# Agent attention fused with a top-1 mixture of experts: two units of keys, and of values, per block of matmuls

## The chip, the core and the metric

The kernel runs on one core of one Trainium2 chip. The metric is device time in microseconds (us) of one execution; lower is better. A core has five engines that each work through a queue of instructions of their own: TensorE (PE, matmuls; PEld is its loading of weights), VectorE (DVE), ScalarE (ACT), GpSimd (POOL) and SyncE (SP, which issues most DMA transfers). [...] Matmul results land in PSUM, which this kernel uses as eight banks of 512 float32 numbers per partition, and ACT or DVE have to read them out before a bank can be written anew.

## The reference, cut to what matters

Four batches of 11456 tokens with 128 channels go through an attention with 49 agents: the agents attend to the keys and average the values, and the queries attend to the agents. The result, 45824 tokens, is the input of a mixture of eight experts of which each token uses one.

```python
def _attn_ref(q, k, v, agents):              # B, N, C = 4, 11456, 128; 49 agents
    scale = 1.0 / np.sqrt(q.shape[-1])
    a2k = softmax(scale * agents @ k.T)      # over the tokens
    agent_v = a2k @ v
    q2a = softmax(scale * q @ agents.T)      # over the agents
    return q2a @ agent_v

def _moe_ref(x, w_gate, w_output_gate, w1, w2):   # E, D, F = 8, 128, 1024
    logits = x @ w_gate
    e_idx = np.argmax(logits, axis=1)
    gate_w = softmax(logits)[np.arange(N), e_idx]
    eom = 1.0 / (1.0 + np.exp(-(x @ w_output_gate)))
    for e in range(E):
        mask = e_idx == e
        h = np.maximum(x[mask] @ w1[e], 0.0)
        out[mask] = gate_w[mask, None] * eom[mask, e, None] * (h @ w2[e])
```

## The kernel before, in words

**Units.** A batch is cut into twelve units: eleven of 1024 tokens (eight sub-tiles of 128) and a short one of 192 (two sub-tiles of 96). A unit of queries, keys or values is loaded by one DMA of 512 KB (96 KB for the short one) into one of seven places in SBUF, and its place comes free when its matmuls are issued. The order of the loads is the list `ITEMS`, and `small_products` handles the items in this order, each only after the one ahead of it has issued its matmuls.

**Keys and values.** For a unit of keys, eight products with the 49 agents and a column of zeros (50 columns in all) give the scores `ks` in one PSUM bank. ACT copies them to SBUF (`S`), DVE keeps a running maximum. When a batch's twelve units are through, the maximum is known, POOL and ACT make the weights `ev` of one unit after another, and eight products of `ev` with the unit's values give its share `av` in a PSUM bank, which DVE adds to the batch's sum (`avs`). When the last unit is added, the batch's average per agent is folded into the first weight matrix of the expert that most of the batch's tokens use. The products of queries (`qs`) give each token's weights over the agents and, through them, its logits.

**The main products.** A tile is half a unit, 512 tokens. Its first products `h` come in two groups (half 0 and half 1), each of four PSUM banks with eight matmuls: four with 128 rows and four with the rest. ACT makes `hh` of each bank (ReLU in 16 bits) and DVE the remainder `hl`; only when DVE is done is the bank free for the next group. The second products `y` add up 16 pairs of matmuls per bank (eight pieces of `hh`, 256 columns wide, and of `hl`, 128 wide, for two sub-tiles), after which ACT (`ys`) and DVE (`os`) read the bank out, POOL multiplies by the gate and SP stores. Banks 0 to 3 belong to `h`; the other four are shared by `y`, scores, values, logits and all small products. Tokens of another expert than the batch's main one are gathered into 14 left-over tiles (`let`, `lx`, `lh`, `ly`) and scattered over the output by an indirect DMA from POOL.

**The order.** The program is straight-line code that is written in the order that a planner finds when the kernel is built. The planner (`Clock`) keeps a modelled time of each engine and tile. `main_stream` (line 1311) picks the next piece of main work: `mm2`, a pair of `y` matmuls, or `mm1`, a group of `h`; where the model can run neither, `idle`. All other work stands in streams, generators that yield what they need next, and `tick` advances those that can run in the model. A matmul of scores or values is cut into pieces of 32 or 64 columns, which run side by side in the column parts of the array. All pieces of a unit are written as one block (`blocked`, line 491), and a block gets a place only in two cases: behind a group of `h` matmuls (`mm1`, line 1226; pieces of `PART` = 32 columns), or in `idle` (line 510; pieces of 64 columns). At most one block is written at such a place.

**Banks.** `bank` takes of the four shared banks the one whose last reader ends first in the model, `hold` and `release` mark it as taken and free. `wait_free(True)` (line 327), which scores use, keeps one bank free for `y` and lets no more than two banks be held by scores at a time:

```python
            keep = clk.started and (long or not (Y or resting[0]))
            if n_free() > keep and not (long and len(long_held) > 1) and first_free()[0] <= clk.now() + 50.0:
                return
```

Up to the first group of `h`, batch 0's keys and values and the first keys of batch 1 are worked through by single matmuls; blocks come into use with the main products. All instructions that the planner writes have line 217 in the profile (`Engine.emit`), so rows are told apart by the names of their tiles.

Of the kernel before, what the change touches and what calls it, by code (L numbers as in the profile page):

```python
# [18 lines left out]
B, N, C, A, E, F = 4, 11456, 128, 49, 8, 1024  # L19
A2 = 50  # L20
NB = F // P
UNITS = [(u * 1024, 128, 8) for u in range(11)] + [(11264, 96, 2)]
# [122 lines left out]
def _free(x):  # L145
    n = 1
    for k in x.shape[1:]:
        n *= k
    return n
# [117 lines left out]
def agent_attention_top1_moe(ctx, tc, qT, kT, v, aT, wg, wo, w1, w2, cst, out):  # L267
# [3 lines left out]
    PE, SY = Engine(clk, "PE", nc.tensor), Engine(clk, "SP", nc.sync)  # L271
# [12 lines left out]
    last = [0]  # L284
# [5 lines left out]
    def n_free():  # L290
        return sum(banks[k][0] for k in others)
# [4 lines left out]
    def first_free():  # L296
        return min((when_free(banks[k]), k) for k in others if banks[k][0])

    def bank(name, dt=F32, w=512, k=None):

        k = last[0] = first_free()[1] if k is None else k
        t = ps.tile([P, w], dt, tag=f"b{k}", bufs=1, name=name)
        banks[k][1] = t.name
        return t

    def hold(long=False):

        k = last[0]
        banks[k][0] = False
        if long:  # L310
            long_held.append((k, banks[k][1]))
        return k

    def release(k):
        banks[k][0] = True
# [11 lines left out]
    def wait_free(long=False):  # L327
        while True:
            long_held[:] = [x for x in long_held if not banks[x[0]][0] and banks[x[0]][1] == x[1]]
# [4 lines that stand above are left out]
            yield None  # L334
# [6 lines left out]
    at = cp.tile([P, B, A2], F32, name="at")  # L341
# [4 lines left out]
    def load_constants():  # L346
        SY.dma_start(kc, cst)
        SY.dma_start(wgo[:, 0:E], wg)
        SY.dma_start(wgo[:, E:2 * E], wo)
        for t in gss:  # L350
            POOL.tensor_copy(t[:, 0, 16:17], own)
        for t in avt:
            POOL.memset(t, 0.0)
        POOL.tensor_tensor(sel, idf[:, 0:A2], idf[:, 64:64 + A2], op=ALU.add)
# [21 lines left out]
    for i in range(4):  # L376
        t = cp.tile([P, 8, P], F16, name=f"e16_{i}")
        e16s.append(t)
    avd = []
    for i in range(2):  # L380
        t = cp.tile([P, P + 32], F32, name=f"avd_{i}")
# [3 lines left out]
    for i in range(2):  # L385
        t = cp.tile([P, 2, 18], F16, name=f"gs_{i}")
# [3 lines left out]
    for i in range(2):  # L390
        t = cp.tile([P, E, NCOL], F32, name=f"oht_{i}")
# [69 lines left out]
    def spawn(g, prio=2):  # L461
        streams.append([prio, len(streams), g, None])
        streams.sort(key=lambda x: x[0])
# [16 lines left out]
    part = [PART]  # L480
# [7 lines left out]
            if x[3] is not None and x[3][0] == "PE" and clk.can(x[3], x[0]):  # L488
                step(x)

    def blocked(o, pairs, last=None):

        yield "PE", list(pairs[0][1:]), [o], 2
        clk.vt["PE"] += TURN
        n = len(pairs)
        for i, (t, x, m) in enumerate(pairs):
            w = _free(x)
            for h in range(0, w, part[0]):
                c = min(part[0], w - h)
                dst = o[h:h + c, :] if last else o[h:h + c, t * A2:(t + 1) * A2]  # L500
                PE.matmul(dst, x[:, h:h + c], m, start=(not last or i == 0), stop=(not last or i == n - 1))
        clk.vt["PE"] += TURN

    def step(x):
# [24 lines left out]
    parts = {}  # L529
# [26 lines left out]
    def scored(item):  # L556
        places[held.pop(item)][0] = True
# [16 lines left out]
    def loads():  # L574
        for n, item in enumerate(ITEMS):
# [5 lines left out]
            if n == 1:  # L581
                load_constants()

    def scores(item, name):

        kind, b, u = item
        base, pp, nt = UNITS[u]
        while item not in parts or urgent[0] or \
                kind == "k" and b == 1 and u >= EARLY and not clk.started:
            yield None  # L590
        yield from wait_free(True)
        x = parts.pop(item)
        s = bank(name)
        mark = hold(True)
        if clk.started:
            yield from blocked(s, [(t, x[:, t * pp:(t + 1) * pp], at[:, b, :]) for t in range(nt)])
            scored(item)
            return s, mark
        for t in range(nt):
            for h in range(0, pp, 64):  # L600
                w = min(64, pp - h)
                yield from PE.q.matmul(s[h:h + w, t * A2:(t + 1) * A2], x[:, t * pp + h:t * pp + h + w], at[:, b, :],
                                       start=True, stop=True)
        scored(item)
        return s, mark

    NU = len(UNITS)


    K = {}  # L610

    def k_unit(b, u):
        if u == 0:
            K[b] = dict(
                S={},
                mx=wk.tile([P, 8, A2], F32, name=f"mx{b}", tag="mx", bufs=1),
                sm=wk.tile([P, 8, A2], F32, name=f"sm{b}", tag="sme", bufs=1),
                k=0, s=0, v=0, av_n=0,
            )
        s, mark = yield from scores(("k", b, u), f"ks{b}_{u}")  # L620
        spawn(k_rest(b, u, s, mark))

    def k_rest(b, u, s, mark):
        base, pp, nt = UNITS[u]
        S, mx = K[b]["S"], K[b]["mx"]

        n = u
        while K[b]["k"] < n:
            yield None
        sv = s[0:pp, 0:nt * A2]  # L630
        if u // 3 not in S:
            S[u // 3] = wk.tile([P, min(24, NCOL - u // 3 * 24), A2], F32, name=f"S{b}_{u}", tag=f"S{u // 3}", bufs=1)
        Su = S[u // 3][0:pp, u % 3 * 8:u % 3 * 8 + nt, :]
        yield from ACT.q.copy(Su.rearrange("p t a -> p (t a)"), sv)
        release(mark)
        if n > 0:
            yield from DVE.q.tensor_tensor(mx[0:pp, 0:nt], Su, S[0][0:pp, 0:nt, :] if n == 1 else mx[0:pp, 0:nt],
                                           op=ALU.max)
        K[b]["k"] += 1
        if n == NU - 1 or b == 0 and n == FIRST - 1:  # L640
            spawn(k_max(b, n), 1)
# [64 lines left out]
    def v_unit(b, u):  # L706
        base, pp, nt = UNITS[u]
        item = ("v", b, u)
        while b not in K or u not in K[b] or item not in parts:
            yield None  # L710
        if b == 0:
            yield from v_turned(u)
            return
        if u == 0:
            K[b]["av"] = wk.tile([P, A2], F32, name=f"avs{b}", tag="avs")
        yield from wait_free()
        avp = bank(f"av{b}_{u}")
        mark = hold()
        avo = avp[:, 0:A2]
        x = parts.pop(item)  # L720
        e = K[b].pop(u)
        yield from blocked(avo, [(t, x[0:pp, t * C:(t + 1) * C], e[:, t, :]) for t in range(nt)], True)
        scored(item)
        K[b]["v"] += 1
        spawn(v_rest(b, u, avo, mark))

    def v_turned(u):

        base, pp, nt = UNITS[u]
        k0 = K[0]  # L730
        if u in (0, FIRST):
            while not any(banks[k][0] for k in range(G4, 8)):
                yield None
            k = min((when_free(banks[k]), k) for k in range(G4, 8) if banks[k][0])[1]
            k0["avp"] = bank(f"avT{u}", k=k), hold()
        avp, mark = k0["avp"]
        x = parts.pop(("v", 0, u))
        e = k0.pop(u)
        for t in range(nt):
            h = t % 2 * 64  # L740
            yield from PE.q.matmul(avp[h:h + A2, 0:C], e[:, t, :], x[0:pp, t * C:(t + 1) * C],
                                   start=(u in (0, FIRST) and t < 2), stop=(u in (FIRST - 1, NU - 1) and t >= nt - 2))
        scored(("v", 0, u))
        k0["v"] += 1
        if u == NU - 4:
            others[:] = range(G4, 8)
        urgent[0] = u == NU - 1
        if u == FIRST - 1:
            k0["old"] = avp, mark
        if u == NU - 2:  # L750
            spawn(v_copy(0, *k0["old"]), 1)
        if u == NU - 1:
            spawn(shares(), -1)
            spawn(v_last(avp, mark), -1)
# [40 lines left out]
    def v_rest(b, u, avo, mark):  # L795
        av = K[b]["av"]
        while K[b]["av_n"] < u:
            yield None
        if u == 0:
            yield from DVE.q.tensor_copy(av, avo)  # L800
        else:
            yield from DVE.q.tensor_tensor(av, av, avo, op=ALU.add)
        release(mark)
        K[b]["av_n"] += 1
        if u == NU - 1:
            spawn(fold(b), -1)

    def averages(b):
# [391 lines left out]
    MIX = [(3, 0)] * 4 + [(0, 0)] + [(0, 2)] * 6 + [(0, 0)]  # L1200
    ITEMS = order()
    UNIT = {"q": q_unit, "k": k_unit, "v": v_unit}
    EARLY = 3
    FIRST = 8
# [587 lines left out]
```

## Time and profile before

| What | Value |
|---|---|
| Time, median of 3 runs | 982.24 us (982.24 to 983.22) |
| Time of the profiled execution | 981.81 us |
| Its span | 980.0 us |
| Granted clock, mean of the span | 0.995 |
| PE busy | 952.6 us (97%) |
| PEld busy | 729.0 us (74%) |
| DVE busy | 788.2 us (80%) |
| ACT busy | 589.7 us (60%) |
| POOL busy | 355.3 us (36%) |
| Moved by DMA | 148.62 MB, mean 152 GB/s |
| Matmuls of `y` with `hh` / with `hl` | 2880 / 2880 |
| Matmuls of `h` | 1472 |

A profile comes from one execution; its time is compared with that execution's span, and the difference between the two lies around the span. Busy times of engines overlap, so they do not add up to the span. A group row of the profile gives the engine, the operation, the tiles (output, arrow, inputs), the count, the busy time, the mean of one in ns, and, behind the second bar, the idle time just ahead of these instructions with what ended it. A row of the timeline begins with the time from the span's start and the duration; `x8` at its end stands for eight instructions of a kind in a row, and a bracket for a wait ahead of it and its releaser.

### The profile page before, as it was taken

The page shows a single profiled execution, that of the slowest core. Times are in us where ns is not written, and L with a number is a line of the kernel's source. Part 1 is how long each engine was busy: PE and PEld are TensorE (multiplying, and loading weights), DVE is VectorE, ACT ScalarE, POOL GpSimd, SP SyncE. Part 2 cuts the span into 40 slices and gives each one's busy share as a digit, 9 for nine tenths or more (in the row PEclk, how much of TensorE's full clock was granted, in tenths as well). Part 3 has the DMA queues.
Part 4 walks back from the last instruction along what each step waited for, and adds up shares of the span by engine and source line. Part 5 has one row for each costly group of instructions (what it writes and reads, how often), then busy time and mean ns, then how long its engine had stood idle before and what let it go on. Part 6 is the DMA issues. An engine that isn't in the chain of part 4 may idle for free. (4 is left out here: it accounts for less than half of the span.)

```text
span 980.0 us, 37550 instructions
## 1 busy us (share of the span) xinstructions
PE 952.6 (97%) x15740; PEld 729.0 (74%) x15740; DVE 788.2 (80%) x2118; ACT 589.7 (60%) x1400; POOL 355.3 (36%) x630
## 2 busy tenths in 40 slices
PE   9999999999999999999999999999999999999994
PEld 7767777777777777777777777777767777877884
DVE  2888978789888888789888888789999878677651
ACT  2366666665756666657666666656566656555551
POOL 1123255451232464432232554522243355443221
PEclk9999999999999999999999999999999999999997
DMA  9996564545566655444557545435343445425420
GB/s 324 306 312 166 163 155 141 167 133 137 155 188 166 156 151 156 149 140 128 164 155 206 148 129 158 128 123 140 89 88 80 154 126 158 149 91 151 138 70 29
DMA packets 108898, 148.62 MB, mean 152 GB/s; under 512 B 62595, under 2 KB 71223, under 8 KB 108725
## 3 DMA queue, kind: packets, MB, share of 16 engines
q1 hardware_dynamic: 107380, 144.70, 50.5%
q8 instruction: 124, 2.03, 0.9%
q0 software_dynamic: 1344, 1.49, 0.8%
q14 instruction: 50, 0.40, 0.1%
HBM read 90.88 MB, written 35.17 MB: 129 GB/s over the span
## 5 line engine op out<-in xcount | busy, mean ns | idle before, releaser
L217 PE MATMUL y<-vv,hh 128*128 128x256 f16 (+1 forms) x2880 | 528.6, 273 | 5.9 <-ACT S L217 1.1
L217 DVE SCALAR_TENSOR_TENSOR hl<-h,hh 128x512 f16<-128x512 f32 (+1 forms) x736 | 449.6, 668 | 100.3 <-ACT hh L217 99.0
L217 PE MATMUL y<-vv,hl 128*128 128x128 f16 (+1 forms) x2880 | 501.3, 219 | 2.4 <-DVE hl L217 1.0
L217 ACT ACTIVATE hh<-h 128x512 f16<-128x512 f32 (+1 forms) x736 | 373.2, 591 | 195.1 <-PE h L217 195.0
L217 PEld LDWEIGHTS <-hh 128*128 128x128 f16 (+1 forms) x2880 | 282.9, 98 | 54.0 <-issue 17.1
L217 PEld LDWEIGHTS <-hl 128*128 128x128 f16 (+1 forms) x2880 | 284.4, 99 | 15.7 <-issue 9.1
L217 PE MATMUL h<-x_ld,w 128*128 128x512 f16 (+1 forms) x1472 | 254.9, 376 | 0.8 <-DVE w L217 0.6
L217 PEld LDWEIGHTS <-w 128*128 128x128 f16 x1472 | 83.3, 95 | 108.3 <-issue 71.6
L217 POOL TENSOR_TENSOR os<-os,smt 128x512 f32<-128x512 f32 (+1 forms) x92 | 98.6, 1071 | 124.5 <-DVE os L217 93.6
L217 ACT COPY ys<-y 128x256 f32<-128x256 f32 x180 | 68.2, 379 | 91.0 <-PE y L217 89.4
L217 DVE TENSOR_TENSOR os<-y,ys 128x256 f32<-128x256 f32 x180 | 75.0, 417 | 34.0 <-ACT ys L217 31.4
L217 POOL TENSOR_TENSOR e<-ef,e 128x392 f16<-128x392 f32 (+1 forms) x48 | 42.0, 876 | 55.6 <-ACT e L217 55.3
L217 POOL TENSOR_TENSOR ev<-S,km_o 128x400 f32<-128x400 f32 (+1 forms) x36 | 32.9, 913 | 60.7 <-PE av L217 58.7
L217 PE MATMUL ks<-at,k_ld 128*32 128x50 f32 (+1 forms) x2348 | 45.9, 213 | 0.9 <-DMA k_ld<-kT 0.9
L217 PEld LDWEIGHTS ks<-at,k_ld 128*32 128x32 f32 (+1 forms) x2348 | 39.5, 116 | 9.5 <-issue 6.9
L217 PE MATMUL qs<-at,q_ld 128*32 128x50 f32 (+1 forms) x2764 | 43.6, 210 | 0.4 <-DMA q_ld<-qT 0.4
L217 PEld LDWEIGHTS qs<-at,q_ld 128*32 128x32 f32 (+1 forms) x2764 | 36.6, 111 | 9.7 <-issue 7.8
L217 PE MATMUL lh<-lxs,lw_ld 128*128 128x128 f32 x224 | 43.4, 276 | 0.1
L217 PE MATMUL ly<-lw_ld,lh 128*128 128x128 f32 x224 | 43.3, 275 | 0.0
L217 POOL TENSOR_TENSOR og<-oh,ll 128x64 f32<-128x64 f32 (+1 forms) x48 | 16.0, 334 | 63.1 <-DVE oh L217 59.6
L217 PEld LDWEIGHTS <-x_ld 128*128 128x128 f16 x360 | 26.2, 97 | 14.7 <-issue 7.1
L217 POOL TENSOR_TENSOR ll<-lL,rr 128x128 f32<-128x128 f32 (+1 forms) x48 | 19.3, 403 | 47.8 <-DVE rr L217 38.5
(250 smaller groups left out, 1003.6 us busy)
## 6 DMA issues: line engine op xcount, KB each, us to landing
v_ld<-v SPq DMA_DIRECT2D x44, 512.0 KB
q_ld<-qT SPq DMA_DIRECT2D x44, 512.0 KB
out<-os SPq DMA_DIRECT2D x88, 256.0 KB
k_ld<-kT SPq DMA_DIRECT2D x43, 512.0 KB
lw_ld<-w SPq DMA_DIRECT2D x28, 512.0 KB
efd<-ef SPq DMA_DIRECT2D x44, 200.0 KB
x_ld<-x_ld SPq DMA_DIRECT2D x132, 64.0 KB
w1t<-w SPq DMA_DIRECT2D x4, 512.0 KB
```

The lines of the kernel that those rows point to most:

```text
L217: return getattr(self.eng, op)(*a, **k)
```

## The change

`blocked` takes several sets of an output and its pairs, and writes all of them as one block.

For keys, once the main products have begun, the even unit of a pair takes its bank, waits until the next unit has landed, takes a second bank and writes both units' products as one block. The second unit's bank is kept in `after`, and when its turn comes, it finds its scores done. Each unit still has its own copy by ACT and its own maximum.

For values, from batch 1 on, the even unit waits for the weights and the values of both units, and writes both as one block that adds up in one bank. DVE adds one sum per two units. The odd unit's own call does nothing. Batch 0 stays as it was.

PE's program goes from 15967 to 15955 rows. There are 18 blocks of values and 18 sums in place of 36, and 16 blocks of two units of keys: (4,5), (6,7), (8,9) and (10,11) of batch 1, whose unit 3 stays alone, and six each of batches 2 and 3.

```diff
-    def blocked(o, pairs, last=None):
-
-        yield "PE", list(pairs[0][1:]), [o], 2
+    def blocked(*sets, last=None):
+
+        outs = {o.name: o for o, _ in sets}
+        yield "PE", [x for _, pairs in sets for x in pairs[0][1:]], list(outs.values()), 2
         clk.vt["PE"] += TURN
-        n = len(pairs)
-        for i, (t, x, m) in enumerate(pairs):
-            w = _free(x)
-            for h in range(0, w, part[0]):
...
+        n = sum(len(pairs) for _, pairs in sets)
+        i = 0
+        for o, pairs in sets:
+            for t, x, m in pairs:
+                w = _free(x)
+                for h in range(0, w, part[0]):
+                    c = min(part[0], w - h)
+                    dst = o[h:h + c, :] if last else o[h:h + c, t * A2:(t + 1) * A2]
+                    PE.matmul(dst, x[:, h:h + c], m, start=(not last or i == 0), stop=(not last or i == n - 1))
+                i += 1
         clk.vt["PE"] += TURN
...
+    after = {}
+
     def scores(item, name):
...
         s = bank(name)
         mark = hold(True)
         if clk.started:
-            yield from blocked(s, [(t, x[:, t * pp:(t + 1) * pp], at[:, b, :]) for t in range(nt)])
+            sets = [(s, [(t, x[:, t * pp:(t + 1) * pp], at[:, b, :]) for t in range(nt)])]
+            if kind == "k" and u % 2 == 0:
+                other = kind, b, u + 1
+                _, pp, nt = UNITS[u + 1]
+                while other not in parts:
+                    yield None
+                yield from wait_free(True)
+                x = parts.pop(other)
+                s1 = bank(f"{name}_1")
+                after[b, u + 1] = s1, hold(True)
+                sets.append((s1, [(t, x[:, t * pp:(t + 1) * pp], at[:, b, :]) for t in range(nt)]))
+            yield from blocked(*sets)
             scored(item)
+            if len(sets) > 1:
+                scored(other)
             return s, mark
...
-        s, mark = yield from scores(("k", b, u), f"ks{b}_{u}")
+        s, mark = after.pop((b, u), None) or (yield from scores(("k", b, u), f"ks{b}_{u}"))
...
     def v_unit(b, u):
         base, pp, nt = UNITS[u]
         item = ("v", b, u)
+        if b > 0 and u % 2:
+            return
         while b not in K or u not in K[b] or item not in parts:
             yield None
         if b == 0:
             yield from v_turned(u)
             return
+        while u + 1 not in K[b] or ("v", b, u + 1) not in parts:
+            yield None
...
-        x = parts.pop(item)
-        e = K[b].pop(u)
-        yield from blocked(avo, [(t, x[0:pp, t * C:(t + 1) * C], e[:, t, :]) for t in range(nt)], True)
+        sets = []
+        for w in (u, u + 1):
+            _, pp, nt = UNITS[w]
+            x, e = parts.pop(("v", b, w)), K[b].pop(w)
+            sets.append((avo, [(t, x[0:pp, t * C:(t + 1) * C], e[:, t, :]) for t in range(nt)]))
+        yield from blocked(*sets, last=True)
         scored(item)
-        K[b]["v"] += 1
+        scored(("v", b, u + 1))
+        K[b]["v"] += 2
         spawn(v_rest(b, u, avo, mark))
...
-        K[b]["av_n"] += 1
-        if u == NU - 1:
+        K[b]["av_n"] += 2
+        if u == NU - 2:
             spawn(fold(b), -1)
```

Since the planner sets the order, the diff does not show where instructions go. Three places on PE follow. In these rows the tile written stands ahead of the arrow, the number behind a name's last underscore only tells tiles apart, and the size is that of one matmul.

**Units 4 and 5 of batch 2's values.** Before, the block of unit 4 stood behind the last `h` matmul of a group, 32 matmuls of 32 columns each (`x32`); unit 5's block of the same form came some 80 rows further on, behind the next group:

```order
L217 MATMUL h_1_2_8762<-x_5_ld,w_0_5726 128x512
L217 LDWEIGHTS w_0_5726
L217 MATMUL h_1_3_8767<-x_5_ld,w_0_5726 128x512
L217 MATMUL av_4_8683<-ev_4_8356,v_4_ld 32x50 x32
L217 LDWEIGHTS hh_0_8432
L217 MATMUL y_1_8825<-vv_0_5729,hh_0_8432 128x256
```

Now both units:

```order
L217 LDWEIGHTS hl_7_8507
L217 MATMUL y_0_8546<-vv_1_5706,hl_7_8507 128x128
L217 MATMUL av_4_8625<-ev_4_8310,v_4_ld 64x50 x16
L217 MATMUL av_4_8625<-ev_5_8333,v_5_ld 64x50 x16
L217 LDWEIGHTS w_2_5747
L217 MATMUL h_1_0_8697<-x_5_ld,w_2_5747 128x512
```

The block has moved from behind a group of `h` to a place between the last `y` and the next `h`, where the planner saw a pause, and its pieces are 64 columns wide instead of 32.

**The half-1 group of `h` of tile 65.** Before, the last matmul of the group and the rows behind it (`ppt` is a small product for the left-over tokens):

```order
L217 LDWEIGHTS w_0_10579
L217 MATMUL h_1_3_15915<-x_9_ld,w_0_10579 128x512
L217 LDWEIGHTS hh_5_15734
L217 MATMUL y_1_15871<-vv_1_10584,hh_5_15734 128x256
L217 MATMUL ppt_15912<-kc,ppi_15857 24x128
L217 LDWEIGHTS hl_5_15735
L217 MATMUL y_1_15871<-vv_1_10584,hl_5_15735 128x128
```

Now:

```order
L217 LDWEIGHTS w_0_10320
L217 MATMUL h_1_3_15641<-x_9_ld,w_0_10320 128x512
L217 LDWEIGHTS hh_0_15563
L217 MATMUL y_0_15660<-vv_0_10323,hh_0_15563 128x256
L217 LDWEIGHTS hl_0_15564
L217 MATMUL y_0_15660<-vv_0_10323,hl_0_15564 128x128
```

Before, `y` work that needs nothing of this group (pieces 5 to 7 of an earlier `y`, then pieces 0 to 3 of the tile's own) stood behind it; now only pieces 0 to 3, eight pairs, are left until the first result of the group, `hl_4`, is read.

**The last left-over tile.** Before, its first product `let` stood inside the last tile's `h` group:

```order
L217 MATMUL h_0_2_21291<-x_11_ld,w_1_15730 128x192
L217 MATMUL let_0_21290<-kc,bigs_0_20753 49x128
L217 LDWEIGHTS w_1_15730
L217 MATMUL h_0_3_21295<-x_11_ld,w_1_15730 128x192
L217 LDWEIGHTS w_0_15709
```

Now it and all that follows from it stand behind the last `y`:

```order
L217 MATMUL y_0_21088<-vv_1_15354,hl_7_21043 96x128
L217 MATMUL let_0_21132<-kc,bigs_0_20586 49x128
L217 MATMUL lx_0_21136<-let_sb_0_21134,lav_0_21081 128x128
L217 MATMUL lh_0_0_21141<-lxs_0_21139,lw_00_0_ld 128x128 x4
L217 MATMUL lh_0_1_21148<-lxs_0_21139,lw_00_0_ld 128x128 x4
L217 MATMUL ly_0_21155<-lw_00_0_ld,lh_0_0_21146 128x128 x4
L217 MATMUL ly_0_21155<-lw_00_0_ld,lh_0_1_21153 128x128 x4
L1753 TENSOR_LOAD more
```

The chain of a left-over tile has moved from among the last `h` and `y` matmuls to the end of PE's program, ahead of the check (`more`) whether further left-over tiles exist.

More of the change, by code (lines that the diff above doesn't have):

```diff
@@ L489, in block @@
                 step(x)
-    def blocked(o, pairs, last=None):
-        yield "PE", list(pairs[0][1:]), [o], 2
+    def blocked(*sets, last=None):
+        outs = {o.name: o for o, _ in sets}
+        yield "PE", [x for _, pairs in sets for x in pairs[0][1:]], list(outs.values()), 2
         clk.vt["PE"] += TURN
-        n = len(pairs)
-        for i, (t, x, m) in enumerate(pairs):
-            w = _free(x)
-            for h in range(0, w, part[0]):
-                c = min(part[0], w - h)
-                dst = o[h:h + c, :] if last else o[h:h + c, t * A2:(t + 1) * A2]
-                PE.matmul(dst, x[:, h:h + c], m, start=(not last or i == 0), stop=(not last or i == n - 1))
+        n = sum(len(pairs) for _, pairs in sets)
[8 more added lines that the diff above has]
+                i += 1
         clk.vt["PE"] += TURN
```

## The prediction

> **What bounds the kernel now.** The page comes first. It gives the span and how full each engine is, and the two groups of second-product matmuls carry the idle time that PE spends ahead of them.
>
> ```profile
> span 980.0 us, 37550 instructions
> PE 952.6 (97%) x15740; PEld 729.0 (74%) x15740; DVE 788.2 (80%) x2118; ACT 589.7 (60%) x1400; POOL 355.3 (36%) x630
> PEclk9999999999999999999999999999999999999997
> L217 PE MATMUL y<-vv,hh 128*128 128x256 f16 (+1 forms) x2880 | 528.6, 273 | 5.9 <-ACT S L217 1.1
> L217 PE MATMUL y<-vv,hl 128*128 128x128 f16 (+1 forms) x2880 | 501.3, 219 | 2.4 <-DVE hl L217 1.0
> ```
>
> PE is busy 97% of 980.0 us at full clock in every slice but the last, so from the first group of h matmuls to the last y matmul the end is set by PE's queue: its instructions, one after another, and the few waits between them. A change to the blocks is therefore worth three things: what PE's instructions cost, the waits that the new order makes, and the tail behind PE. The profiled execution took 981.81 us, 0.43 below the median of 982.24. I add to the former and carry the 0.43 over.
>
> **The blocks themselves.** The timeline of PE shows a group of eight h matmuls that a 32-column block follows, and a group without a block.
>
> ```profile
> 230.60 1.35 PE L217 MATMUL h<-x_ld,w 128*128 128x512 f16 x8
> 231.89 0.92 PE L217 MATMUL av<-ev,v_ld 128*32 128x50 f32 x64
> 232.74 0.28 PE L217 MATMUL y<-vv,hh 128*128 128x256 f16 x1
> ...
> 240.43 1.35 PE L217 MATMUL h<-x_ld,w 128*128 128x512 f16 x8
> 241.71 0.28 PE L217 MATMUL y<-vv,hh 128*128 128x256 f16 x1
> ```
>
> From h to y it is 2.14 us with the block and 1.28 without: a block of one unit costs 0.86. Its 64 records start within 0.92 - 0.21 (one record) = 0.71, which is 11.3 ns a record, so a second unit behind the first costs 64 x 11.3 ns = 0.72. A merged pair in 32 columns saves 0.14. There are 33 merged pairs among the main loop's blocks, so the whole prize is 33 x 0.14 = 4.6 us.
>
> The order takes most of it back. A block that the planner places when neither product can run in its model is cut into 64 columns, and it stands between y and h.
>
> ```profile
> 174.08 0.22 PE L217 MATMUL y<-vv,hl 128*128 128x128 f16 x1
> 174.14 0.27 PE L217 MATMUL y<-vv,hh 128*128 128x256 f16 x1
> 174.25 0.22 PE L217 MATMUL y<-vv,hl 128*128 128x128 f16 x1
> 174.40 1.14 PE L217 MATMUL av<-ev,v_ld 128*64 128x50 f32 x32
> 175.47 0.82 PE L217 MATMUL h<-x_ld,w 128*128 128x512 f16 x3
> ```
>
> From the last y to h it is 1.22 us, against 0.06 from a y to whatever follows it: 1.16 for one unit. A second adds 32 records x (1.14 - 0.22) / 31 = 0.95, so a pair costs 2.11 where 32 columns cost 0.86 + 0.72 = 1.58. No idle time stands ahead of that h, so PE did not need the pause that the planner saw, and I charge all of it. Before: 57 full units alone in 32 columns, 6 in 64, and 6 short units (0.30 each by their 12 or 16 records and the 0.14): 57.8 us. Now: one unit alone in 32, 19 full pairs in 32, three pairs of a full and a short unit in 32 (1.02), nine full pairs in 64 and three mixed ones in 64 (1.46): 57.3. Two more query units run in 64 columns (+0.6). The sum is **+0.1 us**, with bounds of -0.8 and +0.5 for entries and exits that no row of before shows.
>
> **Waits for the h groups' results.** A half-1 group frees its four outputs to y only through ACT and DVE, one after another. At one place the order left too little work between:
>
> ```profile
> 724.11 1.14 PE L217 MATMUL h<-x_ld,w 128*128 128x512 f16 x7
> 725.18 0.28 PE L217 MATMUL y<-vv,hh 128*128 128x256 f16 x1
> 726.51 0.27 PE L217 MATMUL y<-vv,hh 128*128 128x256 f16 x1
> 726.97 0.23 PE L217 MATMUL y<-vv,hl 128*128 128x128 f16 x1 [0.18 <-DVE hl L217]
> 727.20 0.27 PE L217 MATMUL y<-vv,hh 128*128 128x256 f16 x1
> 727.57 0.23 PE L217 MATMUL y<-vv,hl 128*128 128x128 f16 x1
> 725.28 2.06 ACT L217 ACTIVATE hh<-h 128x512 f16<-128x512 f32 x4 [0.77 <-PE h L217]
> 726.24 2.47 DVE L217 SCALAR_TENSOR_TENSOR hl<-h,hh 128x512 f16<-128x512 f32 x4
> ```
>
> Between the group and the first y that reads its hl stand eight y pairs of 0.165 (725.18 to 726.51). DVE delivers an hl every 2.47 / 4 = 0.6, and y eats one per 0.33, so each further one waits 0.26: 0.37 from hh to hl (727.20 to 727.57) instead of 0.11. In the order of before five half-1 groups stand so, with at most eight pairs and no block between; now eight do, two of them with only six pairs, and the main loop's first group loses the second key unit that stood behind it. A place with eight pairs costs 0.58 with DVE on time (0.87 in the rows above, where DVE began late), two pairs fewer another 0.33 and the first group 0.78: 3 x 0.58 + 2 x 0.33 + 0.78 = **+3.2 us**. Bounds: +1.6, if half are covered by other waits, and +4.3 at 0.87 each.
>
> **Waits for PSUM banks.** A pair of key units takes its first bank before its partner has landed and keeps it until the block runs, so y, lg and the small products share what is left of four. By the kernel's own rule for picking a bank, the next tile begins less than 1.1 us of PE time behind the last matmul into its bank at 5 places before and 13 now; the tightest was 0.58 and is 0.06, where the second y of tile 6 follows the first one in the same bank. The nearest row is the end of the last y:
>
> ```profile
> 967.56 0.22 PE L217 MATMUL y<-vv,hl 128*96 128x128 f16 x1
> 967.81 0.37 ACT L217 COPY ys<-y 96x256 f32<-96x256 f32 x1 [2.02 <-PE y L217]
> 968.27 0.42 DVE L217 TENSOR_TENSOR os<-y,ys 96x256 f32<-96x256 f32 x1 [2.02 <-ACT ys L217]
> 968.77 0.61 POOL L217 TENSOR_TENSOR os<-os,smt 96x256 f32<-96x256 f32 x1 [1.40 <-DVE more L217]
> 972.02 0.99 POOL L217 DMA_INDIRECT out<-bigs,ltg_0s  x1 [2.64 <-SPq L1727]
> ```
>
> A y bank is read out 1.13 us behind its last matmul (967.56 to 968.69), a copied-out small product in about half of that (let below: 0.58). Tile 6 waits 1.07. If all places were priced like y, the difference would be 4.4 us; like the fastest, 1.0. Each by its nearest kind I get **+2.0 us**.
>
> [...] This case's rows for the copy and those it holds up:
>
> ```profile
> L217 ACT COPY S<-ks x48: 225/527/555, 7.9 to 537.7; 128x400 f32<-128x400 f32 x44, 96x100 f32<-96x100 f32 x4
>   PE y L217: 1.1, 4
> ```
>
> Only 4 of the main loop's key units held up a y, for 1.1 us of idle together, and the new order reuses a key bank early (under 1.5 us) at two places, as before; so the sum takes nothing for it, and the rival below takes all.
>
> **The tail.** The last left-over tile (let, lx, lh, ly) stood among the last y's. Now it stands behind them all.
>
> ```profile
> 955.05 0.27 PE L217 MATMUL let<-kc,bigs 128*49 128x128 f32 x1
> 955.37 0.26 ACT L217 COPY let_sb<-let 49x128 f32<-49x128 f32 x1 [0.64 <-PE let L217]
> 956.58 0.49 PE L217 MATMUL lx<-let_sb,lav 49*128 49x128 f32 x2
> 957.10 0.27 ACT L217 COPY lxs<-lx 128x128 f32<-128x128 f32 x1 [0.47 <-PE lx L217]
> 961.85 0.60 ACT L217 ACTIVATE lh<-lh 128x512 f32<-128x512 f32 x1 [0.84 <-PE lh L217]
> 964.69 0.39 PE L217 MATMUL ly<-lw_ld,lh 128*128 128x128 f32 x2
> 965.17 0.37 ACT L217 ACTIVATE bigs<-ly,bigs 128x128 f32<-128x128 f32 x1 [2.73 <-PE y L217]
> ```
>
> Two records of such a product take 0.39 with a y pair of 0.165 between them and the next: 0.22 each. So 16 x 0.22 and some 0.6 for let and lx, 4.2 us, leave the stretch that ends with the last y, which comes so much earlier. Behind it the chain runs alone: let to its copy's end 0.6 (0.9 if ys stands ahead of it on ACT), lx and copy 0.9, eight lh 1.8, the second ReLU and its wait 1.0, the four ly that need it 0.9, and 0.7 to the end of ACT: 6.0 to 6.3, and some 0.9 to the scatter, which now waits for it and not for the last store. Before, the scatter came 972.02 - 967.56 = 4.46 behind the last y. The tail changes by 7.1 - 4.46 - 4.2 = about -1.6; I take **-1.3**, with bounds of -2.3 and +1.5 (products not packed at 0.22).
>
> [...]
>
> **What stays.** DVE loses 18 sums (33 to 15), off the path. Loads, queries and the left-over tiles move on SP's queue, but a unit's queries still stand ten or more h groups ahead of their use. I take 0, with 2.5 us either way: waits that come and go when ACT and DVE are late.
>
> **Sum:** 0.1 + 3.2 + 2.0 - 1.3 = +4.0 us on 981.81, so 985.8 in such an execution and **986.2** as the median.
>
> **Rivals.**
> 1. *Waits replace waits.* Every wait of PE lets ACT and DVE catch up, and then later waits vanish (the 8.3 us of idle ahead of the two y groups). For it: most of these idles are single and under 1 us. Against: the three in a row at 726 to 728 come from the order alone. Time: 5.2 us of new waits shrink to 1.2, so 982.24 + 0.1 + 1.2 - 1.3 = 982.2, no change.
> 2. *Faster: the 64-column blocks fill pauses.* If PE must wait for the h banks wherever the planner paused, the twelve pairs in 64 columns cost nothing extra, and the merged turns pay: -4.6 - 1.3, with half of the new waits +2.6, so 979 us. It decides from the point where idle time stands ahead of the h that follows such a block; at 175.47 there is none.
> 3. *Key copies and late evictions bind.* Every one of the 16 key pairs holds up the next bank by one more copy of 0.53: +8.5, and 994 in all; half of it, 990.
>
> **How the numbers follow.** The forecast has a chance of 0.52, the first rival 0.23, the second 0.12, the third 0.13. Under 0.2% (2.0 us) a measurement here cannot be told from no change. Slower by more: nearly all of the forecast and the third, 0.64; same 0.24; faster 0.12. The range reaches from half of the new waits with the best tail, 981.5, to the third rival's half, 990.0. The forecast's own range is 984 to 988.5.
>
> **What would show it.** In the new timeline: pairs as x128 records within 1.5 us in 32 columns; pairs of 64 records between y and h with no idle ahead of h; hl waits behind the half-1 groups of tiles 42, 65, 72 and 73; over 1 us ahead of the second y of tile 6; idle of the two y groups up from 8.3 to 10 or more; and the scatter 6 to 8 us behind the last y. I am wrong if those waits are absent (then 982 or less), or if idle stands ahead of the h's behind the 64-column blocks.

## The result, and the profile after

The changed kernel takes 991.79 us (989.93 to 992.69, 4 runs) where the kernel before takes 982.73 (982.24 to 983.43): a ratio of 1.009 with a 95% interval of 1.0077 to 1.0103. It is 9 us slower. The forecast had the sign, but its 986.2 stood 5.6 us short, and 990.0, the end of the range, was passed. The profiled execution took 992.42 us, 10.6 more than that of before.

The profile's page of the changed kernel, in the order of the rows shown of before, with the row of the instruction queue (packets, MB and share of the DMA engines):

```profile
span 990.7 us, 36411 instructions
PE 956.8 (97%) x15180; PEld 731.1 (74%) x15180; DVE 791.6 (80%) x2100; ACT 587.7 (59%) x1400; POOL 353.9 (36%) x630
q8 instruction: 120, 1.97, 0.8%
L217 PE MATMUL y<-vv,hh 128*128 128x256 f16 (+1 forms) x2880 | 531.0, 273 | 10.5 <-DVE os L217 3.4
L217 PE MATMUL y<-vv,hl 128*128 128x128 f16 (+1 forms) x2880 | 502.6, 219 | 5.4 <-DVE hl L217 2.3
```

The idle time ahead of the two y groups has grown from 8.3 to 15.9 us. Who waited for whom on PE (total, times, longest), in the rows that matter here, after:

```profile
PE y L217 <- DVE os L217: 3.4, 4, 2.1
PE ks L217 <- issue: 2.4, 4, 0.8
PE y L217 <- DVE hl L217: 2.3, 5, 0.8
PE y L217 <- ACT S L217: 2.0, 2, 1.1
PE y L217 <- DVE gs L217: 1.9, 1, 1.9
PE y L217 <- issue: 1.4, 1, 1.4
PE av L217 <- issue: 1.4, 1, 1.4
```

and before, with the row of its instruction queue behind them:

```profile
PE y L217 <- ACT S L217: 1.1, 4, 0.3
PE y L217 <- DVE hl L217: 1.0, 3, 0.4
PE y L217 <- DVE os L217: 0.8, 1, 0.8
PE y L217 <- issue: 0.6, 1, 0.6
```

```profile
q8 instruction: 124, 2.03, 0.9%
```

In the rows with "issue" PE stood still, and nothing that the profile shows had to come first. With 0.3 us inside a block of queries they make 5.5 us, against 0.6 before. PE's timeline shows where: in the middle or at the end of a pair's block, or just behind it.

```profile
159.92 1.64 PE L217 MATMUL av<-ev,v_ld 128*32 128x50 f32 x128
161.49 0.28 PE L217 MATMUL y<-vv,hh 128*128 128x256 f16 x1
...
217.00 1.64 PE L217 MATMUL av<-ev,v_ld 128*32 128x50 f32 x128
220.26 0.23 PE L217 MATMUL y<-vv,hl 128*128 128x128 f16 x1 [1.41 <-issue]
...
365.35 1.63 PE L217 MATMUL av<-ev,v_ld 128*32 128x50 f32 x126
368.39 0.25 PE L217 MATMUL av<-ev,v_ld 128*32 128x50 f32 x2 [1.40 <-issue]
...
494.67 0.99 PE L217 MATMUL ks<-at,k_ld 128*32 128x50 f32 x69
496.43 0.90 PE L217 MATMUL ks<-at,k_ld 128*32 128x50 f32 x59 [0.77 <-issue]
```

The pair at 159.92 ran as it was reckoned. The one at 494.67 stopped after 69 records, though neither its data nor its bank was late.

What came in at these moments is in the DMA records, which list each packet of the instruction queue with its start and duration. (Landing is the sum of the two; "goes on" is the start of PE's next record; times in us.)

```
stopped in or behind   packet began   landed   PE goes on   behind the landing
av pair at 217.00          217.00     218.66     220.26           1.60
ks pair at 282.34          282.17     283.19     284.58           1.39
ks pair at 292.90          292.88     293.84     295.08           1.24
ks pair at 331.15          329.75     330.81     332.31           1.50
av pair at 365.35          365.99     367.14     368.39           1.25
ks pair at 494.67          494.01     494.97     496.43           1.46
qs unit at 500.19          498.70     499.66     501.11           1.45
```

Each stop ended 1.24 to 1.60 us behind the landing of such a packet, and the one wait for "issue" of before, up to 490.17, 1.36 us behind one that landed at 488.81. The queue's 120 packets of 16 KB (1.97 MB), set against PE's 15180 matmuls and 15180 weight loads, make 253 of PE's instructions per packet; before it is 124 packets for 31480, or 254. (A float32 matmul shows as two records with a load each: a unit's 32 matmuls of 32 columns, `x32` in the rows of the order, are `x64` here. It is these records that come out at 253 per packet.) A pair of 128 records and 128 loads in 32 columns takes a whole packet's worth of instructions in 1.4 us, and a packet needs 0.96 to 1.66 us to arrive in these rows (median of all 120: 1.05) and 1.2 to 1.6 more until PE goes on. That is the theory which the runs had to test: **PE ran out of instructions**.

The trace bears it out in one more way. Counted from PE's first one, PE had begun 7618, 9665, 10177, 11714, 13249, 17089 and 17346 instructions when it went on: these numbers lie whole multiples of 256 apart, to within one. So each stop stood exactly where one packet's 256 instructions end and the next packet's begin. Reckoned from there, no packet but the last began more than 286 instructions ahead of the first one that it brings (228 in the median). When a packet began, PE thus had at most some 30 instructions more than one packet's worth left.

### The profile page after: what moved, and what is told of

Read it like the earlier page. It is cut to its first block, busy times and chain, and to the rows that moved or that the text cites. A ratio compares the mean times of both kernels' runs of the same rounds, so it can differ in the third digit from the quotient of the medians.

```text
span 990.7 us, 36411 instructions
## 1 busy us (share of the span) xinstructions
PE 956.8 (97%) x15180; PEld 731.1 (74%) x15180; DVE 791.6 (80%) x2100; ACT 587.7 (59%) x1400; POOL 353.9 (36%) x630
## 3 DMA queue, kind: packets, MB, share of 16 engines
q8 instruction: 120, 1.97, 0.8%
## 5 line engine op out<-in xcount | busy, mean ns | idle before, releaser
L217 PE MATMUL y<-vv,hh 128*128 128x256 f16 (+1 forms) x2880 | 531.0, 273 | 10.5 <-DVE os L217 3.4
L217 POOL TENSOR_TENSOR os<-os,smt 128x512 f32<-128x512 f32 (+1 forms) x92 | 96.2, 1046 | 123.1 <-DVE os L217 83.7
L217 PEld LDWEIGHTS qs<-at,q_ld 128*32 128x32 f32 (+1 forms) x2704 | 36.8, 111 | 10.6 <-issue 8.9
L217 POOL TENSOR_TENSOR sm<-sm,ev 128x400 f32<-128x400 f32 (+1 forms) x33 | 32.2, 975 | 15.1 <-ACT ev L217 14.5
L217 ACT COPY S<-ks 128x400 f32<-128x400 f32 (+1 forms) x48 | 23.0, 488 | 22.3 <-PE ks L217 22.3
```

Of the source, the lines that this page charges most:

```text
L217: return getattr(self.eng, op)(*a, **k)
```

## The experiments

Theory 1 is that one: a pair's block uses up instructions faster than they arrive. Theory 2, the rival at first, is that the gaps are waits for the second unit's data or bank which the trace does not name, and that the loss comes from the held banks and the moved order.

**Two blocks instead of one.** The pairs keep their banks, their loads and their single sum:

```diff
-        yield "PE", [x for _, pairs in sets for x in pairs[0][1:]], list(outs.values()), 2
-        clk.vt["PE"] += TURN
...
         for o, pairs in sets:
+            yield "PE", list(pairs[0][1:]), [o], 2
+            clk.vt["PE"] += TURN
             for t, x, m in pairs:
...
```

> The pairs keep their two banks, their loads and their single sum of values, but the two units' matmuls are written at two places instead of one block. Theory 1 (PE's queue runs dry: a pair's 128 matmuls and 128 weight loads in 1.4 us use up instructions faster than 16 KB packets of them arrive): no step inside a block above 0.1 us, where the changed kernel has eight that sum to 5.5 us; by the order's steps -1.7 and by twice the modelled waits +4.4, some 985.5 us (983.5 to 987.5). Theory 2 (the gaps are waits for the second unit's data or bank, which the trace does not name): gaps of 0.5 us or more remain in or ahead of the second unit's matmuls, and the time stays at 989 or above.

Measured: 983.55 us, a ratio of 1.0008 (0.9998 to 1.0018), no difference from before. The longest step left inside a block is 0.3 us, in a block of queries, where theory 1 had at most 0.1. PE's waits have one row with "issue", and the profile's page shows the two y groups:

```profile
PE y L217 <- issue: 0.5, 1, 0.5
```

```profile
L217 PE MATMUL y<-vv,hh 128*128 128x256 f16 (+1 forms) x2880 | 531.6, 273 | 7.6 <-ACT S L217 1.8
L217 PE MATMUL y<-vv,hl 128*128 128x128 f16 (+1 forms) x2880 | 503.2, 219 | 4.7 <-DVE hl L217 3.0
```

So 8.2 of the 9 us go with writing two units as one block. Banks held in pairs, loads awaited in pairs and 18 sums fewer make no difference that can be measured in this comparison; the last two runs below make one of 3 us. Not all of the 8.2 is the gaps, since the planner's order differs between the two kernels as well.

**Nothing paired, but the blocks of keys written twice.** In the kernel before:

```diff
-            yield from blocked(s, [(t, x[:, t * pp:(t + 1) * pp], at[:, b, :]) for t in range(nt)])
+            yield from blocked(s, [(t, x[:, t * pp:(t + 1) * pp], at[:, b, :]) for t in range(nt)] * (2 if kind == "k" else 1))
```

> The kernel before, in which the matmuls of every block of keys are written twice in a row: 128 records of one unit and one bank, nothing paired, the result the same. The order's steps add 21.3 us. Theory 1: at least three of the doubled blocks have a gap over 0.3 us, each ending 1.2 to 1.7 us behind the landing of an instruction packet, 2 to 7 us in all; 1006 to 1011 us. Theory 2: no gap inside a block, 1004 us (1003 to 1005.5).

Measured: 1012.59 us (1012.12 to 1014.14), above even the first theory's range. Three of the doubled blocks have a gap over 0.3 us (a fourth has 0.27), which ended 1.26, 1.50 and 1.42 us behind the landing of a packet. PE's waits, and one of the three in its timeline:

```profile
PE ks L217 <- issue: 4.6, 3, 2.2
PE y L217 <- issue: 2.9, 4, 1.5
```

```profile
274.59 1.35 PE L217 MATMUL ks<-at,k_ld 128*32 128x50 f32 x102
277.45 0.54 PE L217 MATMUL ks<-at,k_ld 128*32 128x50 f32 x26 [1.52 <-issue]
```

With one unit's data and one bank there is no second unit to wait for, and the gaps come all the same. Theory 2 falls as far as the gaps go.

**64 columns everywhere**, in the changed kernel and in the one before. A unit is then half as many instructions:

```diff
-    part = [PART]
+    part = [2 * PART]
...
-            part[0] = PART
+            part[0] = 2 * PART
```

> The changed kernel with pieces of 64 columns in every block: a pair is 64 matmuls in 1.85 us instead of 128 in 1.43. To be read against the next run, the kernel before with pieces of 64 columns. Theory 1: no step inside a block above 0.2 us, and 0 to 5 us more than the next run (order -4.6, waits +4 to +9), near 1008 us. Theory 2: the gaps stay, 9 us or more above the next run.

> The kernel before with pieces of 64 columns in every block, the partner of the run ahead. The order's steps add 25.7 us: 1008 us (1005 to 1010) under both theories, with no gap inside a block.

Measured: 1004.63 and 1003.39 us. Paired is 1.2 us slower here, not 9, and the intervals of the two (ratios 1.021 to 1.0245 and 1.0193 to 1.0228) overlap. The pairs of keys that stopped at 282.34 and 292.90, and the one ahead of them, in the changed kernel with 64 columns:

```profile
275.99 2.07 PE L217 MATMUL ks<-at,k_ld 128*64 128x50 f32 x64
283.10 2.07 PE L217 MATMUL ks<-at,k_ld 128*64 128x50 f32 x64
293.43 2.07 PE L217 MATMUL ks<-at,k_ld 128*64 128x50 f32 x64
```

None stops, and no wait with "issue" is left on PE. The waits of y stay: their two groups idle for 11.9 us paired and 6.2 single. Both kernels were 3 to 5 us faster than expected, which the runs leave unexplained; the comparison between the two stands.

**One half of the change alone**: keys paired and values as before, and the other way round.

> Only the keys are paired, the values go as before. Theory 1 (instruction supply): the gaps of pairs of keys stay, 2.5 to 4 us, and with waits of twice the modelled +3.9 and the order's -1.0 the time is 985 to 991 us. Rival (the banks that a pair of keys holds cost the most): nearly the whole loss is here, 989 us or more, most of it ahead of the first y of a bank.

> Only the values are paired, the keys go as before. Theory 1: gaps of 1.5 to 3.5 us behind or in pairs of values in 32 columns, 984 to 989 us. Rival (banks of keys): no loss here, 981 to 983.5 us.

Measured: 987.93 us (ratio 1.0054, 1.0034 to 1.0075) with the keys, 986.13 (1.003, 1.0017 to 1.0042) with the values. Each half costs something, so the rival on the banks of keys falls. With the keys PE waits 2.8 us with "issue", 2.2 of it in one block. With the values it is 0.2 us only, where 1.5 to 3.5 were expected: there the loss is in the waits of y (12.6 us of idle ahead of its two groups, 4.3 more than before), which I put down to the moved order; no run tried that.

**32 columns everywhere**, in the changed kernel and in the one before:

```diff
-            part[0] = 2 * PART
+            part[0] = PART
```

> The changed kernel with pieces of 32 columns also where the planner saw a pause. The order's steps take 6.3 us less than in the changed kernel, but twelve pairs more are 128 records in 1.43 us. Theory 1: the gaps grow from 7 us to 9 to 14, and most of the gain is lost: 987 to 992 us. Rival (gaps come from single places, not from how dense a block is): gaps stay at 7 us, 985 us or less.

> The kernel before with pieces of 32 columns everywhere; all blocks are of one unit, 64 records in 0.71 us. The order's steps take 2.2 us less. Theory 1: a single unit's block does not run dry, since its 128 instructions are half a packet: 980.8 us (979.5 to 982). Rival: where the planner pauses PE waits anyway, so a shorter block gains nothing: 982.5 to 983.5 us.

Measured: 1000.72 us (996.18 to 1001.69) and 985.33 us (983.1 to 986.74). In the changed kernel the steps of its order are 6.3 us shorter, and it takes 9 us more, far above what either theory said. Its waits:

```profile
PE ks L217 <- issue: 3.9, 2, 3.2
PE av L217 <- issue: 2.6, 2, 2.2
PE y L217 <- issue: 2.2, 4, 1.4
PE h L217 <- issue: 0.9, 2, 0.4
```

With the queries' 0.5 that is 10.1 us. A second price shows in the kernel before with 32 columns, first a gap in PE's timeline, then the windows around it (window, busy time of PE, PEld, DVE, ACT and POOL with counts, granted clock, DMA share, GB/s):

```profile
60.24 0.90 PE L217 MATMUL ks<-at,k_ld 128*32 128x50 f32 x61
64.44 0.38 PE L217 MATMUL ks<-at,k_ld 128*32 128x50 f32 x3 [3.30 <-issue]
```

```profile
55.00:63.60 8.60, 5.40 (x218) 3.78 (x217) 6.84 (x17) 4.96 (x10) 1.19 (x3) 1.00 1.04 406
63.60:70.40 6.80, 5.96 (x83) 3.29 (x87) 2.56 (x6) 2.85 (x6) 0.00 (x0) 0.50 0.88 298
```

PE stood for 3.3 us, and from 63.6, still within that stop, the granted clock was 0.50 for 6.8 us. In the changed kernel with 32 columns everywhere it was halved four times before the end, for 17.1 us in all (the first time, for 3.4 us, at 10.9, ahead of any block). The expectation of the kernel before was wrong: blocks of one unit can run dry too. This one came soon after two more units without a break (128 records at 57.84), while loads filled the DMA engines (share 1.04, 406 GB/s); its packet began at 61.83, when PE had been standing for 0.7 us. That the loads held the packet up is argued from this and was not tried.

**32 columns only where that place is past.**

```diff
-            part[0] = 2 * PART
+            part[0] = PART if clk.now() > 70e3 else 2 * PART
```

> The run with pieces of 32 columns in all blocks of the kernel before lost 3.5 us in one gap of a block at 60.9 us and some 2.8 us to the halved clock behind it. Here the pieces in the planner's pauses stay at 64 columns until 70 us of the planner's time and are 32 wide from there on (seven units fewer in 64 columns than in the kernel before). Theory 1 (that gap came from the density of instructions at that place): no gap over 0.8 us and no halved clock before the end; the order's steps take 1.35 us less, 981.5 us (980.5 to 982.5). Rival (the shorter blocks gain nothing, since PE would wait there anyway): 982.5 to 983.5 us.

Measured: 980.31 us, a ratio of 0.9972 (0.9961 to 0.9983). No clock was halved before the end, but one gap of 1.1 us is left in a block of values at 177, so the bound of 0.8 was missed. The gain is twice the order's 1.35. The last two runs take this up and let the planner count an `hl` as ready 300 ns later:

```diff
-                can2 = len(vv) > f // 4 and clk.at([H[i, f][1], vv[f // 4]]) <= now
+                can2 = len(vv) > f // 4 and clk.at([H[i, f][1], vv[f // 4]]) <= now - 300.0
```

> The run before, and the planner counts an hl as ready 300 ns later than it did, so that y stands further behind the group that it reads. The modelled waits for hl fall from 2.9 to 2.5 us, those for banks rise from 1.6 to 1.9. If the waits for late hl's are a cost of their own: 979.5 to 981.5 us. If they only take the place of others: as the run before.

> Units paired in banks, loads and sums but written as two blocks, with the two edits of the two runs before. Theory 1: no dense block, so nothing runs dry; the order's steps and modelled waits give -2.2 us against the kernel before and -2.7 against the two-block version: 980.8 us (979 to 983). Rival (a pair's two held banks cost something of their own): 983 us or more, with the waits ahead of the first y of a bank above 9 us.

Measured: 979.46 us without pairs, a ratio of 0.9965 (0.9953 to 0.9977), and 982.49 (0.9997, 0.9988 to 1.0006) with units paired in two blocks. The first is faster than both kernels, and PE's waits have no row with "issue". That the margin itself gains anything is not shown, since its interval covers that of the run ahead of it. The paired one is 3 us behind it, and these two intervals do not overlap, so with hardly a stop (one of 0.3 us in a block of queries) pairing still costs something here. Its y group with hh, which holds the first y of each bank, idles for 6.6 us (6.2 without pairs), where the rival had above 9, and 982.49 is short of its 983, so the rival as stated is not confirmed. But the waits of y behind the key copies have grown from 1.1 to 2.9 us, and those for hl from 1.3 to 2.9. The rows of the paired one:

```profile
PE y L217 <- DVE hl L217: 2.9, 6, 1.2
PE y L217 <- ACT S L217: 2.9, 4, 1.2
```

Pairing gains nothing here either.

## Why the prediction was wrong

Its steps against the profiled executions, +4.0 forecast and +10.6 measured:

- **The blocks, +0.1.** This is the step that failed. "A second unit behind the first costs 64 x 11.3 ns" took the pace of a single unit's 64 records for one that PE can hold over 128. It can, when the packets happen to fall well (1.43 us from the first to the last record at 159.92); where they do not, a pair stands for 0.3 to 1.4 us. The bounds of -0.8 and +0.5 covered the entry and the exit of a block, not its supply. By the waits it is 5.5 - 0.6 = **+4.9 us**. The profile of before had a trace of it, one wait of y for "issue" of 0.6 us that ended at 490.17, and its row of the instruction queue; the prediction used neither. Where one packet followed another inside a dense block, PE stood for up to 3.3 us (the kernel before with 32 columns).
- **Waits for hl and for banks, +5.2.** Right in kind and nearly in size. Without "issue" the two y groups idle for 7.7 us before and 14.5 after, **+6.8**; paired and single in 64 columns differ by 5.7. By the profile's rows 2.6 of it are waits for `os` (a bank), 1.3 for `hl` and 0.9 for `S`; 1.9 is one wait for `gs`, which the prediction did not name. The hl waits stand at 469 to 479, 689 to 699 and 739 to 768, around the tiles that were named. The second y of tile 6 was priced at 1.07 us, with DVE on time. It took 2.14, since the bank's `os` stood behind four `hl` of a group on DVE:

```profile
129.77 0.27 PE L217 MATMUL y<-vv,hh 128*128 128x256 f16 x1 [2.14 <-DVE os L217]
...
126.90 2.48 DVE L217 SCALAR_TENSOR_TENSOR hl<-h,hh 128x512 f16<-128x512 f32 x4 [0.66 <-ACT hh L217]
129.30 0.41 DVE L217 TENSOR_TENSOR os<-y,ys 128x256 f32<-128x256 f32 x1
```

- **A halved clock, not in the sum.** Behind 1.90 us of idle, which ended at 254.77, the clock was 0.50 for 3.4 us from 255.2 on:

```profile
254.77 0.27 PE L217 MATMUL y<-vv,hh 128*128 128x256 f16 x1 [1.90 <-DVE gs L217]
```

```profile
255.20:258.60 3.40, 3.40 (x21) 2.60 (x18) 1.70 (x5) 0.53 (x1) 0.00 (x0) 0.50 0.84 227
```

  y pairs then came every 0.32 us instead of 0.165, by which I estimate a loss of 1 to 1.7 us over the stretch. The sum has no term for the clock. Behind the last y it stayed 1.00 until PE was done (976.20 to 981.80).
- **The tail, -1.3.** Right: the scatter came 982.51 - 976.20 = 6.31 us behind the last y, 1.85 more than before, and 4.2 us of work left the stretch ahead of it, so -2.3, the bound.

```profile
976.20 0.22 PE L217 MATMUL y<-vv,hl 128*96 128x128 f16 x1
979.77 2.01 PE L217 MATMUL ly<-lw_ld,lh 128*128 128x128 f32 x16
...
982.51 1.04 POOL L217 DMA_INDIRECT out<-bigs,ltg_0s  x1 [4.49 <-ACT bigs L217]
```

These make 0.1 + 4.9 + 6.8 + 1 - 2.3 = 10.5 of the 10.6 us. That it comes out so close is luck in part: the blocks' 0.1 stands here as forecast, the clock is an estimate, and waits that the sum leaves out have gone (1.3 us of `ga` for DVE, 0.9 of keys and 0.4 of queries for their loads), so something that the sum does not name must have grown by about as much. The prediction's "2.5 us either way" for everything else was there for such things.

Three slips in the prediction's working change nothing: it speaks of 33 merged pairs where its own list has 34, its three places at 0.87 with the other two terms make 4.1 where it has 4.3, and half of the new waits with the best tail make 982.6 where its range begins at 981.5.

The rivals: key copies did not bind in the changed kernel (y waited 2.0 us for S, 1.1 before). The 64-column blocks filled no pause, since PE's waits have none ahead of the h behind them. "Waits replace waits" fits in part: with the pairs as two blocks the y groups idle for 4.0 us more than before, but PE as a whole (span less busy time) only 28.3 us against 27.4, and the time is the same.

What stays open is why some packets began late, so that PE had little or nothing left, and how much of the 8.2 us between one block and two is the gaps themselves, how much the late DVE and the halved clock that they and the order bring.

## What to carry to other kernels

Count the instructions of a dense stretch, not only its matmul time: here 256 of PE's instructions inside 1.4 us were as many as one packet brings, and a merge that should save 0.14 us of entry and exit then costs up to 1.4. A wait that the profile puts down to "issue" on the engine that sets the time is worth a look at the instruction queue's packets, and the remedies that took the stops away here were to spread such blocks between slower work (0.5 us of "issue" left with two blocks) or to make the pieces larger (none left, but with 64 columns everywhere the kernel before took 20 us longer). Stalls of PE can cost more than themselves: the clock was halved behind some of 1.9 to 3.3 us, for 3.4 or 6.8 us.

## What the runs showed of the hardware

- PE's instructions arrive in packets of 16 KB, 253 to 254 matmuls and weight loads each, in all thirteen kernels. Where PE ran dry, it went on 1.2 to 1.6 us behind a packet's landing, and a multiple of 256 instructions from the other stops, to within three (to within one in the changed kernel). This holds for all 33 waits with "issue" of 0.18 us or more between 55 us and the last y, in nine kernels alike.
- The clock was halved for 3.4 us (from 255.2 in the changed kernel), or for 6.8 (from 63.6 in the one before with 32 columns), at the end of some of PE's stalls or soon behind them (1.90, 2.2 and 3.3 us long, in the changed kernel, the one with keys alone and the one before with 32 columns), and not behind another of such a length (2.14 us, up to 129.77 in the changed kernel, where it stayed 1.00 until 255.2). So the length of a stall alone did not decide; what did is not shown.
